# Where SyncE takes the branch over a path that isn't taken: a planned RWKV and expert kernel on one core

## The chip, the cores and the metric

The kernel runs on one core of a Trainium2 chip. The core has a matrix engine (TensorE, "PE" in the profile), three engines for elementwise work (VectorE "DVE", ScalarE "ACT", GpSimd "POOL") and SyncE ("SP"), which in this kernel issues nearly every DMA transfer. Each engine runs its own instructions in order and waits for the others by semaphores. The metric is the device time of one execution in microseconds.

## The reference

Three stages follow each other: a linear attention with decay over the sequence, and two feed-forward stages over the tokens that come out of it.

```python
B, H, S, D = 4, 8, 768, 48
for t in range(S):                                   # attention
    kt, vt, rt = k[:, :, t], v[:, :, t], r[:, :, t]
    cur = einsum('bhd,bhe->bhde', u[None] * kt, vt)
    y[:, :, t] = einsum('bhd,bhde->bhe', rt, state + cur)
    state = w[None, :, :, None] * state + einsum('bhd,bhe->bhde', kt, vt)
x = y.transpose(0, 2, 1, 3).reshape(3072, 384)
h = maximum(maximum(x @ w1, x @ w2), x @ w3)         # 384 -> 768
x = h @ w_out                                        # 768 -> 384
g = x @ w_gate                                       # 384 -> 1536
out = (silu(g) * (x @ w_val)) @ w_out2               # 1536 -> 384
```

All arrays are float32. The decays w are drawn between 0.85 and 0.95.

## The kernel before

The sequence is cut into 6 blocks of 128 tokens; with 4 batch entries there are 24 chunks, numbered n. A chunk of the first block (n below 4) needs no state: its products of queries and keys ("s n"), a masked selection ("select n") and the product with the values ("y n") give its output, and a further product of keys and values ("u n") its contribution to the state. From n = 4 on one step of TensorE, "h n", makes the scores of chunk n and the outputs of chunk n - 1. Between these steps TensorE runs the first feed-forward stage of the blocks that are done ("m i f j", "o i c q") and then the whole second stage ("g", "e").

Each product of a feed-forward stage is made of three passes in a reduced format, from a high and a low part of each operand. The weights are split on the chip, piece by piece (jobs k = 0, 1, ...): "fetch k" brings a piece (SyncE, line 226, into one of three "raw" tiles), "scale k" and "sign k" read it on ScalarE (lines 235, 242), "top k" and "rest k" on VectorE (lines 275, 281; rest k is the last reader of the raw tile, and fetch k + 3 waits for it), "hi k" (ScalarE, line 286) and "lo k" (GpSimd or VectorE, line 289) write the two parts. Pieces 2f and 2f + 1 belong to row f of the first weights, w_a.

The data of a chunk come by SyncE: "load n" brings queries and keys (line 313, four transfers for n from 4 on), scaled by VectorE in "scaled n" (line 352); "rows n" brings keys, values and queries in natural order (line 335, four transfers), used by GpSimd in "bonus n" (lines 365, 366) and "keys n" (line 370). For the first four chunks the keys in natural order come by load_keys (line 341). "sided" (lines 776, 777) copies a table of powers in four transfers, "ub" (line 730) brings u in two, and four transfers (line 725) copy another table into Pz.

The kernel also has a general path for decays outside a range, a loop over the sequence on VectorE that is not taken here. Each engine reads a flag from memory (line 800) and branches over that code (line 801). The flag is made by two instructions of VectorE (lines 780, 781, the step "flag").

The order of all this is not written by hand. A planner (class Plan) holds for each step the engines that can do it, with a cost, its needs, a lag until its result is there, and sometimes an earliest time ("at"). It takes step after step: among those whose needs are planned it takes the one with the least start time less 0.08 times the length of work that depends on it, and calls the function that writes its instructions. Program order on each engine is the order in which the planner took the steps. An engine's first free time stands in the planner's start values; for SyncE it is 20.0. What SyncE issues before that is written ahead of the planner: the loads of the first four chunks, fetch 0 to 2, the copies into Pz, rows 4, the keys of the first four chunks and ub. In the planner those count as there at fixed times:

```python
add(("fetch", k), {"none": 0.0}, [], lambda e: None, at=15.0 + 1.8 * k)
add(("keyed", n), {"none": 0.0}, [("turned",)], lambda e: None, at=20.0 + 0.7 * n)
add(("rows", n), {"none": 0.0}, [], lambda e: None, at=18.0)
```

The step "branch" belongs to no engine. It is taken when the blanked tile, the outputs of the first four chunks, their fills and the flag are planned, and it writes the branch into all five engines at that point of their order. On SyncE the planner had by then placed sided, fetch 3 and load 4.

Of the kernel before, what the change touches and what calls it, by code (L numbers as in the profile page):

```python
# [20 lines left out]
B, H, S, D = 4, 8, 768, 48  # L21
# [69 lines left out]
class Plan:  # L91
# [8 lines left out]


    SHARED = ("top", "rest", "lo", "xlo", "ylo", "prod", "p2", "choose")

# [11 lines left out]
    def run(self, idle, hop=0.1):  # L115
        steps, free = self.steps, self.free
        users, waits = {k: [] for k in steps}, {}
        for key, (_, needs, *_) in steps.items():
# [29 lines left out]
        while ready:  # L148
# [20 lines left out]
            if e == "pe":  # L169
                idle(start - free[e], k)  # L170
            steps[k][2](e)
            free[e] = start + cost
# [11 lines left out]
def rwkv_moe(ctx: ExitStack, tc: tile.TileContext, qk, nat, kn, vn, rn, wcol, wh, uh, wup1, wout1, wup2, out):  # L184
# [459 lines left out]
    with tc.manual_schedule():  # L644
# [77 lines left out]
        for z in range(2):  # L722
            for x in range(2):

                nc.sync.dma_start(out=Pz[64 * z:64 * z + D, 2 * x:2 * x + 2], in_=P129[64 * x:64 * x + D, 2 * z:2 * z + 2])
        load_sides(B)
        for n in range(B):
            load_keys(n)
        for x in range(2):
            nc.sync.dma_start(out=ub[64 * x:64 * x + 64],  # L730
                              in_=uh[NPAIR * x:NPAIR * x + NPAIR].unsqueeze(0).to_broadcast([64, NPAIR, D]))

# [37 lines left out]
        def turned(_):  # L770
            nc.scalar.copy(PT.rearrange("p (j a) d -> p j a d", a=2), late["pt"][:, :, :, 0:D])

        def sided(_):
# [92 lines left out]

        plan = Plan(dict(pe=6.4, dve=5.7, act=6.5, pool=3.3, sync=20.0, none=0.0), order)
        add = plan.add
# [51 lines left out]
        add(("turned",), {"act": 0.5}, [("p", 0)], turned)  # L920
        add(("powers z",), {"act": 0.75}, [("scaled", B - 1)], powers_z, at=16.0)
        add(("sided",), {"sync": 2.0}, [("turned",)], sided, lag=3.0)
        for n in range(B):
            add(("load", n), {"none": 0.0}, [], lambda e: None, at=5.8 + 2.35 * n)
            add(("keyed", n), {"none": 0.0}, [("turned",)], lambda e: None, at=20.0 + 0.7 * n)
            add(("prod", n), {"pool": 1.3} if n > 1 else {"dve": 0.68}, [("load", n)] + ([("d", n - 2)] if n > 1 else []),
                lambda e, n=n: product_columns(n, engine[e]))
            add(("d", n), {"pe": 0.68}, [("prod", n)] + ([("a0", n - 1)] if n else []), lambda e, n=n: diagonal(n))
            add(("scaled", n), {"dve": 1.23}, [("prod", n)], lambda e, n=n: prep_scores(n))
            add(("keys", n), {"pool": 1.03}, [("keyed", n), ("low", B - 1)], lambda e, n=n: prep_keys(n))  # L930
            add(("s", n), {"pe": 1.1}, [("scaled", n)] + ([("select", n - 1)] if n else []), lambda e, n=n: scores(n))
            add(("a0", n), {"act": 0.17}, [("d", n)], lambda e, n=n: bonus(n, engine[e]))
            for x in range(2):
                add(("fill", n, x), {"pool": 1.05, "act": 1.28}, [("a0", n)],
                    lambda e, n=n, x=x: fill(n, x, engine[e]))
            add(("select", n), {"dve": 1.27}, [("s", n), ("fill", n, 0), ("fill", n, 1)], lambda e, n=n: select(n))
            add(("y", n), {"pe": 1.6}, [("select", n)] + {0: [("turned",)], 2: [("low", 0)]}.get(n, bank_free["y", n]),
                lambda e, n=n: apply(n))
            add(("row", n), {"act": 0.48}, [("y", n)], lambda e, n=n: upper(n))
            add(("low", n), {"dve": 0.58}, [("row", n)], lambda e, n=n: lower(n))  # L940
            add(("u", n), {"pe": 0.6}, [("y", n), ("keys", n), ("branch",)] + bank_free["u", n], lambda e, n=n: outer(n))
            add(("update", n), {"act": 0.37}, [("u", n)], lambda e, n=n: update(n))
        for n in range(B, NB * B):
            i, last = n // B, n >= (NB - 1) * B

            done = [("h", n - 1)] if n > B + 1 else []
            add(("load", n), {"sync": 1.9}, done or [("s", n - B)], lambda e, n=n: load_columns(n), lag=2.5,
                at=0.0 if done else 17.0 + 2 * n - 2 * B)
            space = [("rows", B)] if n == B + 1 else [("u", n - B - 2)] if n in (B + 2, B + 3) else [("h", n - 2 if n < 11 else n - 1)] if n > 2 * B else []
            if n > B:  # L950
                add(("rows", n), {"sync": 2.4}, space, lambda e, n=n: load_sides(n), lag=2.5, at=17.0 if n < 2 * B else 40.0)
            else:
                add(("rows", n), {"none": 0.0}, [], lambda e: None, at=18.0)
            add(("bonus", n), {"pool": 2.05}, [("rows", n), ("rest", 2)], lambda e, n=n: prep_bonus(n, engine[e]))
            add(("scaled", n), {"dve": 1.35}, [("load", n), ("low", B - 1), ("lo", 1), ("powers z",)], lambda e, n=n: prep_scores(n))
# [17 lines left out]
        rows0 = [("low", n) for n in range(B)]  # L973
        add(("flag",), {"dve": 0.35}, [("s", 1)], flag, lag=3.0)
        for i in range(2, FAR):
# [157 lines left out]
```

## Time and profile before

| what | value |
|---|---|
| median of 3 runs | 837.82 us (835.02 to 838.01) |
| the profiled execution's own time | 836.52 us |
| its span, first to last instruction | 834.8 us |
| mean granted TensorE clock | 0.995 |
| TensorE busy | 814.4 us, 98% |
| VectorE, ScalarE, GpSimd busy | 362.5, 314.3, 143.0 us |
| moved by DMA | 74.00 MB, 89 GB/s over the span |

The profile is of one execution. Busy times are sums over the span; for TensorE a busy share of 98% leaves 2% of gaps, and where these lie must be read from views with a place or a time. The time of an execution is 1.7 us longer than its span.

### The profile page before, as it was taken

To read this page: it belongs to the slowest core of one execution; us is meant where nothing else is said; L and a number is where in the kernel's file an instruction comes from. 1 tells how busy PE (TensorE), PEld (TensorE's weight loads), DVE (VectorE), ACT (ScalarE), POOL (GpSimd) and SP (SyncE) were. 2 spreads that over 40 slices of the span, in tenths; PEclk is the share of its full clock that TensorE was granted. 3 is DMA by queue.
4 is the path that set the end of the run, shared out by engine and by line. 5 is a ranking of instruction groups with operands and counts; after the bars stand their busy time and mean duration, and the time that the engine had idled before them with its cause. 6 is when DMAs were issued, how large, how long until landed. Compare 5 with 4: busy or idle time off the path is not lost.

```text
span 834.8 us, 14481 instructions
## 1 busy us (share of the span) xinstructions
PE 814.4 (98%) x6058; PEld 673.1 (81%) x6058; DVE 362.5 (43%) x552; ACT 314.3 (38%) x641; POOL 143.0 (17%) x146
## 2 busy tenths in 40 slices
PE   9978899999999999999999999999999999999998
PEld 8756678888888888888888888888888888888886
DVE  7789846747556543234572322222231222213121
ACT  5677753555535432234672211221231122113111
POOL 5763513334343420000121000000000000000000
PEclk9999999999999999999999999999999999999999
DMA  9795725465564462321230100100010010001001
GB/s 268 200 234 147 256 84 146 151 196 166 153 218 136 140 203 104 136 110 58 85 114 1 38 0 1 38 0 1 1 38 0 1 38 0 1 1 39 0 1 38
DMA packets 43787, 74.00 MB, mean 89 GB/s; under 512 B 4584, under 2 KB 30504, under 8 KB 42952
## 3 DMA queue, kind: packets, MB, share of 16 engines
q1 hardware_dynamic: 43712, 73.06, 28.5%
q8 instruction: 47, 0.77, 0.4%
q14 instruction: 20, 0.16, 0.1%
q10 hardware_dynamic: 8, 0.00, 0.0%
HBM read 57.51 MB, written 14.16 MB: 86 GB/s over the span
## 4 chain that ended last, share of the span: by engine, by line
PE 89%; DMA 4%; issue 3%; POOL 2%; SPq 1%; ACT 0%; DVE 0%; POOLq 0%; DVEq 0%; ACTq 0%
PE g L567 12%; PE g L569 12%; PE g L568 12%; PE m L567 8%; PE m L569 8%; PE m L568 7%; PE oo L569 6%; PE oo L567 6%; PE oo L568 6%; PE o L567 3%; PE o L569 3%; PE o L568 3%; PE s L483 2%; PE y L483 2%; DMA raw<-in_wup 1%
## 5 line engine op out<-in xcount | busy, mean ns | idle before, releaser
L567 PE MATMUL g<-xhi,w_c 128*128 128x512 f32 x432 | 168.0, 389 | 0.0
L568 PE MATMUL g<-xlo,w_c 128*128 128x512 f32 x432 | 168.0, 389 | 0.0
L569 PE MATMUL g<-xhi,w_c 128*128 128x512 f32 x432 | 168.0, 389 | 0.0
L624 DVE TENSOR_TENSOR g<-mm,g 128x512 f32<-128x512 f32 x72 | 50.1, 696 | 257.1 <-PE g L569 256.4
L567 PE MATMUL m<-xhi,w_a 128*128 128x512 f32 x324 | 129.6, 400 | 2.0 <-ACT t L235 2.0
L569 PE MATMUL m<-xhi,w_a 128*128 128x512 f32 x324 | 127.6, 394 | 1.5 <-DVE w_a L289 1.3
L568 PE MATMUL m<-xlo,w_a 128*128 128x512 f32 x324 | 127.3, 393 | 0.2 <-DVEq L801 0.2
L620 ACT ACTIVATE mm<-g 128x512 f32<-128x512 f32 x72 | 43.0, 597 | 151.7 <-PE g L569 151.7
L569 PEld LDWEIGHTS g<-xhi,w_c 128*128 128x128 f32 x432 | 81.1, 188 | 16.9
L568 PEld LDWEIGHTS g<-xlo,w_c 128*128 128x128 f32 x432 | 81.1, 188 | 16.8
L567 PEld LDWEIGHTS g<-xhi,w_c 128*128 128x128 f32 x432 | 81.1, 188 | 16.8
L629 ACT CAST gs<-g 128x512 fp32r<-128x512 f32 x72 | 42.2, 587 | 134.0 <-DVE g L624 134.0
L567 PE MATMUL oo<-gs,w_c 128*128 128x512 f32 x216 | 84.0, 389 | 0.0
L568 PE MATMUL oo<-gs,w_c 128*128 128x512 f32 x216 | 84.0, 389 | 0.0
L569 PE MATMUL oo<-gs,w_c 128*128 128x512 f32 x216 | 84.0, 389 | 0.0
L567 PEld LDWEIGHTS m<-xhi,w_a 128*128 128x128 f32 x324 | 61.5, 190 | 15.6 <-ACT t L235 2.1
L569 PEld LDWEIGHTS m<-xhi,w_a 128*128 128x128 f32 x324 | 61.5, 190 | 15.3 <-DVE w_a L289 1.7
L568 PEld LDWEIGHTS m<-xlo,w_a 128*128 128x128 f32 x324 | 61.5, 190 | 12.7 <-DVEq L801 0.5
L601 DVE TENSOR_TENSOR gs<-g,gs 128x512 fp32r<-128x512 f32 x72 | 49.8, 691 | 43.1 <-ACT gs L629 43.1
L598 ACT CAST hs<-m 128x512 fp32r<-128x512 f32 x33 | 19.3, 584 | 78.8 <-DVE m L586 78.8
L568 PEld LDWEIGHTS oo<-gs,w_c 128*128 128x128 f32 x216 | 40.5, 188 | 8.4
L569 PEld LDWEIGHTS oo<-gs,w_c 128*128 128x128 f32 x216 | 40.5, 188 | 8.4
(135 smaller groups left out, 1153.2 us busy)
## 6 DMA issues: line engine op xcount, KB each, us to landing
raw<-in_wup SPq DMA_DIRECT2D x36, 576.0 KB, 4.8
nat<-in_nat SPq DMA_DIRECT2D x80, 144.0 KB, 3.3
aside<-parts SPq DMA_DIRECT2D x12, 576.0 KB, 4.1
w_c<-aside SPq DMA_DIRECT2D x6, 1152.0 KB, 5.8
qk<-in_qk SPq DMA_DIRECT2D x39, 128.0 KB, 3.0
out<-ob SPq DMA_DIRECT2D x18, 256.0 KB, 2.1
qk<-in_qk SPq DMA_DIRECT2D x41, 96.0 KB, 2.7
raw<-in_wout SPq DMA_DIRECT2D x6, 384.0 KB, 3.8
```

The lines of the kernel that those rows point to most:

```text
L483: nc.tensor.matmul(to, w, x, **(how or dict(start=True, stop=True)))
L567: nc.tensor.matmul(p, wh_, xh, start=first, stop=False)
L568: nc.tensor.matmul(p, wh_, xl, start=False, stop=False)
L569: nc.tensor.matmul(p, wl_, xh, start=False, stop=last)
L598: nc.scalar.copy(hsplit[i, f][0], banks["m", i, f, 2])
L601: nc.vector.tensor_tensor(out=g[1], in0=p, in1=g[0].bitcast(F32), op=ALU.subtract)
L620: nc.scalar.activation(out=hs[i, f], in_=banks["g", i, f, 0], func=AF.Silu)
L624: nc.vector.tensor_tensor(out=p, in0=hs[i, f], in1=p, op=ALU.mult)
L629: nc.scalar.copy(t[:, 0], banks["g", i, f, 1])
```

## The change

Four edits belong together.

- SyncE's transfers rows 4, the keys of the first four chunks and ub are no longer written ahead of the planner but are steps of it, with costs on SyncE (2.4, 0.8 each, 0.6) and a lag of 2.5. What needs them waits for them: keys n for keyed n, bonus n for rows n and ub.
- Until the branch is planned, the planner takes SyncE's steps but keeps back their instructions ("held"). When it takes the branch it writes the branch first, and then what was held, in the order in which it was taken. So in SyncE's program order the branch stands directly behind the copies into Pz.
- A step of another engine that needs a step of SyncE also needs the branch (FENCE), so that its instructions are written behind those of the transfer.
- The flag is planned when scaled 0 is, not s 1. SyncE's first free time in the planner is 17.3, not 20.0, and load n from 4 on has no earliest time any more.

```diff
+    FENCE = ("branch",)
...
     def run(self, idle, hop=0.1):
         steps, free = self.steps, self.free
+        held = []
+        for _, (on, needs, *_) in steps.items():
+            if "sync" not in on and any("sync" in steps[d][0] for d in needs):
+                needs.append(self.FENCE)
...
-            steps[k][2](e)
+            if e == "sync" and self.FENCE not in done:
+                held.append((steps[k][2], e))
+            else:
+                steps[k][2](e)
+            if k == self.FENCE:
+                for do, on in held:
+                    do(on)
...
-        load_sides(B)
-        for n in range(B):
-            load_keys(n)
-        for x in range(2):
-            nc.sync.dma_start(out=ub[64 * x:64 * x + 64],
-                              in_=uh[NPAIR * x:NPAIR * x + NPAIR].unsqueeze(0).to_broadcast([64, NPAIR, D]))
...
+        def bring_bonus(_):
+            for x in range(2):
+                nc.sync.dma_start(out=ub[64 * x:64 * x + 64],
+                                  in_=uh[NPAIR * x:NPAIR * x + NPAIR].unsqueeze(0).to_broadcast([64, NPAIR, D]))
...
-        plan = Plan(dict(pe=6.4, dve=5.7, act=6.5, pool=3.3, sync=20.0, none=0.0), order)
+        plan = Plan(dict(pe=6.4, dve=5.7, act=6.5, pool=3.3, sync=17.3, none=0.0), order)
...
+        add(("ub",), {"sync": 0.6}, [], bring_bonus, lag=2.5)
         add(("sided",), {"sync": 2.0}, [("turned",)], sided, lag=3.0)
...
-            add(("keyed", n), {"none": 0.0}, [("turned",)], lambda e: None, at=20.0 + 0.7 * n)
+            add(("keyed", n), {"sync": 0.8}, [], lambda e, n=n: load_keys(n), lag=2.5)
...
-            add(("keys", n), {"pool": 1.03}, [("keyed", n), ("low", B - 1)], lambda e, n=n: prep_keys(n))
+            add(("keys", n), {"pool": 1.03}, [("keyed", n), ("turned",), ("low", B - 1)], lambda e, n=n: prep_keys(n))
...
-            add(("load", n), {"sync": 1.9}, done or [("s", n - B)], lambda e, n=n: load_columns(n), lag=2.5,
-                at=0.0 if done else 17.0 + 2 * n - 2 * B)
+            add(("load", n), {"sync": 1.9}, done or [("s", n - B)], lambda e, n=n: load_columns(n), lag=2.5)
...
-            if n > B:
-                add(("rows", n), {"sync": 2.4}, space, lambda e, n=n: load_sides(n), lag=2.5, at=17.0 if n < 2 * B else 40.0)
-            else:
-                add(("rows", n), {"none": 0.0}, [], lambda e: None, at=18.0)
-            add(("bonus", n), {"pool": 2.05}, [("rows", n), ("rest", 2)], lambda e, n=n: prep_bonus(n, engine[e]))
+            add(("rows", n), {"sync": 2.4}, space, lambda e, n=n: load_sides(n), lag=2.5, at=17.0 if n < 2 * B else 40.0)
+            add(("bonus", n), {"pool": 2.05}, [("rows", n), ("ub",), ("rest", 2)], lambda e, n=n: prep_bonus(n, engine[e]))
...
-        add(("flag",), {"dve": 0.35}, [("s", 1)], flag, lag=3.0)
+        add(("flag",), {"dve": 0.35}, [("scaled", 0)], flag, lag=3.0)
```

## Rows read from the trace of the kernel before

**Rows 1.** The page, part 1: busy time and share of each engine.

```profile
PE 814.4 (98%) x6058; PEld 673.1 (81%) x6058; DVE 362.5 (43%) x552; ACT 314.3 (38%) x641; POOL 143.0 (17%) x146
```

**Rows 2.** Timeline of TensorE: start, length, instruction, idle before it and its releaser.

```profile
36.26 0.50 PE L569 MATMUL m<-xhi,w_a 128*128 128x512 f32 x1 [1.28 <-DVE w_a L289]
...
47.57 0.47 PE L567 MATMUL m<-xhi,w_a 128*128 128x512 f32 x1 [2.04 <-ACT t L235]
...
63.51 0.29 PE L483 MATMUL s<-nat 64*64 64x48 f32 x4 [3.40 <-DVE am L415]
...
106.22 0.37 PE L483 MATMUL y<-am,nat 64*48 64x64 f32 x2 [3.83 <-issue]
```

**Rows 3.** Four stretches: length, busy times, granted clock, DMA share, GB/s.

```profile
15.20:28.00 12.80, 12.61 (x157) 10.35 (x154) 10.69 (x15) 10.67 (x24) 8.89 (x8) 1.00 0.80 211
28.00:32.50 4.50, 4.50 (x22) 3.72 (x21) 4.47 (x5) 2.65 (x4) 4.50 (x4) 1.00 0.43 107
32.50:61.40 28.90, 24.10 (x323) 18.45 (x321) 20.92 (x30) 19.36 (x50) 17.99 (x14) 0.94 1.01 239
112.00:800.00 688.00, 688.00 (x4682) 569.81 (x4681) 266.41 (x399) 235.37 (x460) 84.13 (x83) 1.00 0.22 71
```

**Rows 4.** Timeline of SyncE's DMA issues.

```profile
8.16 4.35 SPq L725 DMA_DIRECT2D Pz<-P  x4
12.56 4.96 SPq L335 DMA_DIRECT2D nat<-in_nat  x4
17.56 2.59 SPq L341 DMA_DIRECT2D kv<-in_nat  x4
20.19 1.13 SPq L730 DMA_DIRECT2D ub<-in_uh  x2
...
24.64 0.52 SPq L226 DMA_DIRECT2D raw<-in_wup  x1
25.26 2.54 SPq L313 DMA_DIRECT2D qk<-in_qk  x4
31.52 0.34 SPq L226 DMA_DIRECT2D raw<-in_wup  x1
...
35.21 2.49 SPq L313 DMA_DIRECT2D qk<-in_qk  x4
```

**Rows 5.** Line 800, the flag read: engine, length in ns, first and last start.

```profile
L800 SPq TENSOR_LOAD <-slow_i x1: 722/722/722, 27.9 to 27.9; - x1
```

**Rows 6.** Line 801, the branch, in the same columns.

```profile
L801 SPq EVENT_SEMAPHORE  x8: 17/17/17, 29.5 to 31.4; - x8
...
L801 DVEq EVENT_SEMAPHORE  x1: 21/21/21, 27.0 to 27.0; - x1
```

**Rows 7.** DMA issues from 25.2 to 27.8: KB each, median us to landing.

```profile
qk<-in_qk SPq DMA_DIRECT2D x2, 128.0 KB, 4.1
qk<-in_qk SPq DMA_DIRECT2D x2, 96.0 KB, 4.1
```

**Rows 8.** Timeline of VectorE.

```profile
10.32 1.32 DVE L417 COPY_PREDICATED am<-mask,s 128x1024 f32<-128x1024 uint8 x1 [1.15 <-ACT am L403]
...
25.81 1.17 DVE L281 SCALAR_TENSOR_TENSOR t<-raw,t 128x576 uint16<-128x576 uint32 x1
...
31.42 1.26 DVE L352 TENSOR_TENSOR qk<-qk,powers_z 112x512 f32<-112x512 f32 x2
...
35.47 0.74 DVE L289 TENSOR_TENSOR w_a<-t,w_a 128x576 fp32r<-128x576 f32 x1
...
43.41 1.29 DVE L352 TENSOR_TENSOR qk<-qk,powers_z 112x512 f32<-112x512 f32 x2 [6.14 <-DMA qk<-in_qk]
44.61 0.75 DVE L275 SCALAR_TENSOR_TENSOR t<-t,signs 128x576 uint32<-128x576 uint32 x1
```

**Rows 9.** The chain that ended last, up to 26 us: start, length, what.

```profile
5.97 9.18 DMA raw<-in_wup
...
23.81 2.48 POOL kv L370 x2
```

**Rows 10.** The tile Pz: its transfers from issue to landing.

```profile
DMA to landing us min/median/max: 6.0/7.4/9.0
```

## The prediction

> **What bounds the kernel now.** I read the page first. TensorE is busy for 814.4 of the 834.8 us [rows 1], so only its gaps can give time back, 20.4 us in all. TensorE's instructions in order of time show the large ones behind the first up product [rows 2]: 1.3 us in front of an up product at 36.26, waiting for a weight; 2.0 us in front of one at 47.57; 3.4 us in front of a state step at 63.51; 3.8 us, called issue, that end at 106.22. From 112 to 800 us it is busy without a gap (the fourth of [rows 3]), so a microsecond that TensorE gains before that is a microsecond of the total, and one that it doesn't gain is nothing.
>
> Next the other stretches of that view, for DMA and the clock [rows 3]. From 32.5 to 61.4 us the DMA share is 1.01: the engines are full. Before that they aren't: 0.80 over 12.8 us and 0.43 over the 4.5 us from 28.0 to 32.5, which is 2.6 us unused in each. The granted clock of 32.5 to 61.4 is 0.94, so some products there run at the lower level (1.2 GHz): 28.9 x 0.06 = 1.7 us, behind the 2.0 us gap.
>
> Then SyncE's queue in order of time [rows 4]. It issues with little rest up to 27.8 us, and then nothing until 31.52, when fetch 4 goes out, although the tile that fetch 4 refills was read for the last time at 26.98 (rest 1 on VectorE, 25.81 + 1.17, [rows 8]). The hole is the branch: SyncE loads the flag at 27.9 [rows 5] and its eight semaphore events run from 29.5 to 31.4 [rows 6]. The last transfers before the hole are load 4's four, issued 25.26 to 27.80 and landing 4.1 us after issue each [rows 4, 7]: from 29.4 to some 31.4. The events start and end just there. So I read the hole as SyncE, inside the branch that isn't taken, waiting until each of its outstanding transfers has landed.
>
> Last, VectorE [rows 8]: it stands 6.14 us from 37.27 to 43.41 for load 5, which SyncE issued at 35.21. Behind it in VectorE's order are top 4 (44.61) and rest 4, then hi 4 and lo 4, the weight of the up product that starts at 47.57. That is the chain from the hole to TensorE: branch, fetch 4, rows 5, fetch 5, load 5, scaled 5, top 4, lo 4, TensorE.
>
> **The change, part by part.** *The flag* is planned after scaled 0, not after s 1: its two instructions, among VectorE's smallest, move ahead of select 0, in front of which VectorE idles 1.15 us at 10.32 [rows 8]. That wait hides them; without it they would cost their own length once, the same that they cost now. I take 0.
>
> *SyncE's branch* comes right behind the four Pz transfers. Their issues end at 12.5. From the flag's load to the first event took 1.6 us (27.9 to 29.5), so the events begin near 14.1; then SyncE must see raw 0 to 2 and Pz land. Raw lands at 15.15 [rows 9]. Pz landed 6.0 to 9.0 us after issue, the last one (issued 12.0) at about 18.0 [rows 10], but then with nat's transfers behind it on the engines. So SyncE is through between 15.2 and 18.1; I take 17.0, nearer to the upper end, since Pz queues behind raw.
> The Trainium skill, page "Runtime: NRT & Kernel Launch", Instruction fetch mechanics, says that a taken branch to code outside the fetched pages must first fetch it by DMA. By that rule the step from 12.5 to the first event could be longer here than at 28 us, since the engines are full at 13 us; no row of before shows SyncE branching under load, and the sum would stay within the upper end.
>
> *What is now behind it.* By the planner's weights I expect this order from 17.0: rows 4 (four transfers, 2.54 us as load 4 took), keys 0 and 1 (half of 2.59), ub 1.13, fetch 3 0.52, the four sided transfers (from the end of ub at 21.3 to 24.6, 3.3), load 4 2.54 [rows 4]: 11.3, with the gaps between issues 11.5. Fetch 4 then goes out at 28.5, not at 31.52: 3.0 us sooner. With 15.2 and 18.1 in place of 17.0 it is 4.5 (rest 1's own limit as well) and 1.9 sooner. Keys 2 and 3 probably follow rows 5 and take the 1.3 us that they no longer take before load 4, so load 5 is 1.7 to 3.0 us sooner. Before, rows 4 took 4.96 us for the same four issues, being held up by full engines; that time now passes inside the branch. This is why a wait of 3.6 us moved to a start 4.4 us later still gains.
>
> *The other engines.* Steps that need a transfer of SyncE must follow the branch. Everything so bound already stood behind it: VectorE's event is at 27.0 [rows 6], and keys 0 on GpSimd at 23.81 [rows 9] is the earliest such step. Cost 0, since the transfers land in time: rows 4 are issued by 19.5 and keys 0 by 20.2, and at the 4.1 us of load 4 they are there by 24.3, which is 0.5 us late for keys 0 at worst, and GpSimd idles for several microseconds before lo 3. Load 4 is the tight one: its last transfer is issued at about 28 and lands near 31.7, where scaled 4 starts at 31.42 [rows 8]. Between 1.5 us sooner and 1.4 later (P at 15.2 and 18.1), and lateness goes on to lo 2 (35.47 to 36.21, [rows 8]), for which TensorE already waits 1.3 us. I take 0.3 lost, which the 2.0 us gap absorbs.
>
> *What TensorE gets.* If load 5 lands 1.7 to 3.0 us sooner, the 2.0 us gap that begins at 45.5 is gone or nearly so, and with it most of the 1.7 us of low clock: TensorE can be 2 to 3.7 us ahead at 51.7. The next gap, 3.4 us before 63.51, waits for load 6. That one is issued when h 5 has run on TensorE, so it moves along, but it lands through full engines. How far ahead they are is bounded by the share they leave unused. Before: 5.2 us up to 32.5. After: about 1.5 idle until P, and 2.3 MB issued over 11.5 us is 202 GB/s against 239 GB/s when full [rows 3], so 0.15 x 11.5 = 1.8 unused; together 3.3 to 3.8. That leaves 1.4 to 1.9 us from this side and 3.0 from the issue side.
> The Trainium skill, page "Trainium Kernel Development and Optimization", Key Constraints, speaks against the change: transfers of all queues share the same 16 engines, and other ways of issuing only save the sequencer's time. By that rule the gain would be the 1.4 us of share recovered; by the issue side alone 3.0.
> Behind 61.4 the engines are no longer full, and what is gained stays. I take 2.5 us, between the two sides and nearer to the issue side, since the 2.0 us gap itself hangs on load 5, ahead of most of the full stretch.
>
> Sum: the profiled execution took 836.52 us (span 834.8 and 1.7 around it); 836.5 - 2.5 = **834.0 us**. The median of the runs shown is 1.3 us above the profile; on its scale it is 835.3.
>
> **The rivals.**
> *Bigger.* VectorE's order changes: in the new plan load 5 is due later, so top 4 and rest 4 may stand ahead of scaled 5. Then w_a2 waits for no load, fetch 7 (behind rest 4) goes out up to 5 us sooner, the backlog in front of load 6 is less, and part of the 3.4 us gap goes too: 2.0 + 1.7 + up to 3.4 = 7, or 829.5 to 832. For it: load 5's lateness is the planner's error in before. Against: load 6 still waits for h 5. The issue gap of 3.8 us before 106.22 is the other piece that could go if TensorE reaches it while the engines are less full; it hangs on relative timing that the change hardly touches.
> *Nothing.* The full engines give back all of it: load 6 lands as late as now, and TensorE waits 5 us there. For it: share 1.01 until 61.4. Against: 2.6 us unused just at the hole. 836 to 837.
> *Slower.* SyncE's events aren't waits for its own transfers but for the other engines to be through their branch. VectorE's event is at 27.0 [rows 6], so SyncE would stand from 14 to 27 with nothing in flight, and fetch 4 would be issued at 38.5, 7 us later than now: 841 to 845. It decides from the point at which SyncE leaves after 20.0 (31.5 less 11.5). For it: VectorE was through before SyncE's first event. Against: GpSimd works behind its branch at 23.81 [rows 9], before VectorE has come to its own; and the four waits match four landings. A milder form with the same sign is keys 2 and 3 running on GpSimd at 35 beside rest 3 and lo 2 on VectorE, 2.5 us for the pair as for keys 0 and 1 [rows 9]; it costs 1 to 2 us at the 1.3 us wait.
>
> **How the numbers follow.** Forecast 0.44, bigger 0.30, nothing 0.12, slower 0.14. About 0.5%, 4.2 us, is what a measurement of this kernel can tell from no change. Of the forecast's own range (832 to 835.5) a tenth lies beyond that, so faster 0.34, same 0.52, slower 0.14. The range leaves out the strongest bigger case and the slower one: 829.5 to 838.
>
> **What would show it.** SyncE's flag load near 12.6 us and its events ending by 18.1, with no hole at 28; fetch 4 near 28.5; VectorE's wait for load 5 shorter than 4.5 us, or top 4 ahead of it; no TensorE gap before 47.57 and no products at the lower clock behind it; the gap before h 6 still there. The prediction is wrong if SyncE's events end near 27, if scaled 4 starts after 33, or if the gap before h 6 grows by what the one before it lost.

## The result and the profile after

The changed kernel takes 829.8 us (median of 5 runs, 828.58 to 831.98), the kernel before 837.82 us in the same series (835.02 to 839.17). The ratio is 0.9914, with a 95% interval of 0.9888 to 0.994: about 7 us faster. The profiled execution took 829.47 us, its span is 827.8 us. So 7.0 us are to be found between the two traces.

Part 1 of the page after, to be read beside [rows 1]:

```profile
PE 811.8 (98%) x6058; PEld 671.1 (81%) x6058; DVE 361.1 (44%) x550; ACT 314.8 (38%) x645; POOL 143.8 (17%) x147
```

TensorE is busy 2.6 us less for the same 6058 instructions, since fewer of them run at the lower clock, and idle 4.4 us less (16.0, was 20.4). The timeline of TensorE after has these large gaps up to h 6, in the columns of [rows 2]; from 100 to 112 us it shows none:

```profile
36.66 0.50 PE L581 MATMUL m<-xhi,w_a 128*128 128x512 f32 x1 [1.99 <-DVE w_a L301]
...
46.43 0.47 PE L579 MATMUL m<-xhi,w_a 128*128 128x512 f32 x1 [0.52 <-DVE h L598]
...
53.48 0.50 PE L581 MATMUL m<-xhi,w_a 128*128 128x512 f32 x1 [1.39 <-DVE w_a L301]
...
57.99 0.50 PE L581 MATMUL m<-xhi,w_a 128*128 128x512 f32 x1 [0.77 <-DVE w_a L301]
...
62.44 0.42 PE L495 MATMUL s<-nat 64*64 64x48 f32 x4 [2.56 <-POOL nat L377]
```

The 2.0 us gap of before is down to 0.52, the one ahead of h 6 to 2.56, and the 3.83 us inside h 9 (called issue) are gone. Two waits for weights between h 5 and h 6, 1.39 and 0.77 us, are new. A fourth gap of before, ahead of h 8, is gone too; it ended 0.10 us behind a step of VectorE (a "select", line 415), which after runs 4.75 us sooner, ahead of other work:

```profile
82.27 0.71 DVE L415 COPY_PREDICATED am<-mask,s 128x512 f32<-128x512 uint8 x1
...
83.08 0.25 PE L483 MATMUL s<-nat 64*64 64x48 f32 x2 [1.20 <-issue]
```

```profile
77.52 0.74 DVE L427 COPY_PREDICATED am<-mask,s 128x512 f32<-128x512 uint8 x1
```

Where TensorE stood at the same step of its work, from the start times of these timelines, gives the ledger (us; "not held" is an experiment below):

```
step                         before   after   lead   not held, 2nd   its lead
h 4                           38.09   38.47   -0.4       39.84         -1.8
h 5                           51.70   48.67    3.0       49.82          1.9
h 6                           63.51   62.44    1.1       63.66         -0.2
h 7                           73.48   73.14    0.3       74.40         -0.9
h 8                           83.08   81.56    1.5       82.82          0.3
h 9                          100.32   98.94    1.4       99.78          0.5
first up product behind h 9  106.52  100.94    5.6      101.79          4.7
h 10                         120.41  113.41    7.0      114.26          6.2
```

At h 7 the lead is down to 0.3 us; 1.2 us come with the gap ahead of h 8, so that 1.4 us are there at h 9. 4.2 us come inside h 9 and 1.4 us behind it: 5.6 us in a place that the forecast left as it was. These are two executions, and one kernel's executions differ by as much as the early leads: a second profile of the kernel before reached h 7 at 76.40 and h 9 at 103.80. Over the profiles of all experiments below (without the two with added transfers), h 7 starts at 73.48 to 76.40 in the old order and at 72.72 to 74.79 in the new one, so a lead there isn't shown. The gap ahead of h 8 (1.08 to 1.52 us) stands in all five profiles of the old order and in none of the new one. The stages, in the columns of [rows 3]; the third row here is a new one:

```profile
15.20:28.00 12.80, 12.80 (x158) 10.64 (x157) 10.09 (x13) 10.52 (x24) 7.05 (x7) 1.00 0.59 167
28.00:32.50 4.50, 4.50 (x21) 3.73 (x20) 4.02 (x4) 2.75 (x4) 3.74 (x3) 1.00 0.64 156
...
16.50:20.10 3.60, 3.60 (x50) 3.09 (x48) 2.28 (x4) 3.02 (x9) 0.94 (x1) 1.00 0.00 1
...
32.50:61.40 28.90, 22.72 (x321) 17.19 (x320) 23.22 (x32) 20.22 (x51) 16.19 (x14) 1.00 1.01 260
100.00:112.00 12.00, 12.00 (x118) 10.03 (x109) 7.60 (x15) 8.31 (x20) 2.66 (x2) 1.00 0.61 198
112.00:800.00 688.00, 688.00 (x4682) 569.78 (x4681) 265.79 (x397) 235.29 (x459) 83.36 (x82) 1.00 0.22 71
```

SyncE's hole hasn't vanished, it has moved: from 16.5 to 20.1 us the DMA engines move nothing at all. What they leave unused from 15.2 to 32.5 us is 12.8 x 0.41 + 4.5 x 0.36 = 6.9 us, against 5.1 before. The low clock of 32.5 to 61.4 is gone from there, but a stretch of it stands behind the gap ahead of h 6, where the kernel before had the full clock (the first line is of after, the second of before):

```profile
62.44:65.80 3.36, 3.36 (x126) 3.36 (x128) 3.22 (x5) 1.76 (x3) 3.36 (x4) 0.50 0.07 22
```

```profile
62.00:66.00 4.00, 2.49 (x130) 2.40 (x131) 3.97 (x8) 1.88 (x4) 0.00 (x0) 1.00 0.29 112
```

So of the two stretches at the lower level that the kernel before has up to 112 us, one moved and one went: in 100 to 112 the clock was 0.86 before, with 8.17 us busy of 12, and is 1.00 after:

```profile
100.00:112.00 12.00, 8.17 (x148) 6.50 (x147) 4.80 (x9) 5.03 (x12) 2.15 (x3) 0.86 0.60 198
```

SyncE's DMA issues after [rows 4], and its flag read and events, with VectorE's event [rows 5, 6]:

```profile
8.11 4.03 SPq L737 DMA_DIRECT2D Pz<-P  x4
18.64 2.60 SPq L347 DMA_DIRECT2D nat<-in_nat  x4
21.29 1.07 SPq L353 DMA_DIRECT2D kv<-in_nat  x2
22.41 1.12 SPq L781 DMA_DIRECT2D ub<-in_uh  x2
23.65 0.50 SPq L238 DMA_DIRECT2D raw<-in_wup  x1
24.20 1.49 SPq L787 DMA_DIRECT2D PT<-PT  x1
...
27.70 2.79 SPq L325 DMA_DIRECT2D qk<-in_qk  x4
30.60 0.52 SPq L238 DMA_DIRECT2D raw<-in_wup  x1
31.17 2.51 SPq L347 DMA_DIRECT2D nat<-in_nat  x4
33.73 1.07 SPq L353 DMA_DIRECT2D kv<-in_nat  x2
34.90 0.36 SPq L238 DMA_DIRECT2D raw<-in_wup  x1
35.37 2.52 SPq L325 DMA_DIRECT2D qk<-in_qk  x4
```

```profile
L811 SPq TENSOR_LOAD <-slow_i x1: 742/742/742, 12.2 to 12.2; - x1
...
L812 SPq EVENT_SEMAPHORE  x8: 17/17/17, 18.0 to 18.6; - x8
...
L812 DVEq EVENT_SEMAPHORE  x1: 21/21/21, 26.7 to 26.7; - x1
```

The order is the one of the forecast, the start isn't: rows 4 at 18.64, fetch 4 at 30.60, load 5 at 35.37 (35.21 before). Load 4's transfers take 3.4 and 2.8 us to land, against 4.1 [rows 7]:

```profile
qk<-in_qk SPq DMA_DIRECT2D x2, 128.0 KB, 3.4
qk<-in_qk SPq DMA_DIRECT2D x2, 96.0 KB, 2.8
```

VectorE after, around its wait for load 5 [rows 8]: lo 3, top 4, rest 4, and then scaled 5:

```profile
37.58 0.75 DVE L301 TENSOR_TENSOR w_a<-t,w_a 128x576 fp32r<-128x576 f32 x1
38.24 0.76 DVE L287 SCALAR_TENSOR_TENSOR t<-t,signs 128x576 uint32<-128x576 uint32 x1
39.03 1.49 DVE L293 SCALAR_TENSOR_TENSOR t<-raw,t 128x576 uint16<-128x576 uint32 x1
44.14 1.28 DVE L364 TENSOR_TENSOR qk<-qk,powers_z 112x512 f32<-112x512 f32 x2 [3.62 <-DMA qk<-in_qk]
```

Load 5 is there 0.7 us later than before. The wait is shorter because three instructions moved in front of it; before, top 4 stood behind it at 44.61. The chain that ended last no longer reaches back to 26 us [rows 9]; it starts with an issue gap at 90.74 and this row:

```profile
90.83 0.57 DVE w_b L301
```

Pz lands about as long after its issue as before [rows 10]; its last transfer, issued at 11.64, lands at 18.02:

```profile
DMA to landing us min/median/max: 6.4/7.6/8.7
```

### The profile page after: what moved, and what is told of

The parts are those of the page before. It is cut to its first block, busy times and chain, and to the rows that moved or that the text cites. A ratio compares the mean times of both kernels' runs of the same rounds, so it can differ in the third digit from the quotient of the medians.

```text
span 827.8 us, 14490 instructions
## 1 busy us (share of the span) xinstructions
PE 811.8 (98%) x6058; PEld 671.1 (81%) x6058; DVE 361.1 (44%) x550; ACT 314.8 (38%) x645; POOL 143.8 (17%) x147
## 4 chain that ended last, share of the span: by engine, by line
PE 89%; ACT 0%; DVE 0%; issue 0%
PE g L579 12%; PE g L580 12%; PE g L581 12%; PE m L579 8%; PE m L580 7%; PE m L581 7%; PE oo L579 6%; PE oo L581 6%; PE oo L580 6%; PE o L581 3%; PE o L579 3%; PE o L580 3%; PE s L495 2%; PE y L495 2%; ACT ob L653 0%; DVE w_b L301 0%
## 5 line engine op out<-in xcount | busy, mean ns | idle before, releaser
L581 PEld LDWEIGHTS m<-xhi,w_a 128*128 128x128 f32 x324 | 60.8, 188 | 18.1 <-DVE w_a L301 5.4
```

The lines of the kernel that those rows point to most:

```text
L581: nc.tensor.matmul(p, wl_, xh, start=False, stop=last)
```

## The experiments

Each ratio is to the kernel before in the same series, with its 95% interval.

**A second profile of the kernel before** (no edit), to see whether the gap inside h 9 is an accident of one execution.

> The kernel before, unchanged, for a second profile. Theory C (most of the difference is a gap of TensorE of 3.8 us at 102.4 that belongs to the kernel before): the gap is there again, 3 to 4.5 us long inside the tenth chunk's step, with a block of TensorE's code landing at its end and products at the lower clock behind it; span 834 to 837. Rival (the gap was an accident of one execution): no gap at 102, span 829 to 831.

The gap is there again: 3.55 us ahead of 109.43, called issue (841.02 us, one execution).

**The old order with the early branch.** Only SyncE's program differs from the kernel before; the order planned for the other engines is untouched.

```diff
+            if e == "sync" and ("branch",) not in done:
+                held.append((steps[k][2], e))
...
-        load_sides(B)
-        for n in range(B):
-            load_keys(n)
...
+        plan.first = first_transfers     # rows 4, keys 0 to 3, ub: first of what was held
```

> The kernel before with SyncE's branch directly behind the copies into Pz, and rows 4, the keys, ub, sided, fetch 3 and load 4 behind it in the old order; every other engine's program is that of before. Theory A (the early branch pays by itself): fetch 4 goes out 1 us or more sooner than at 31.52 and TensorE is at least 1 us ahead at 98 us; 1 to 2 us less if the gap at 102 stays, 6 to 7 less if it goes. Theory B (the planner's new order on VectorE and GpSimd gave what was gained before 98 us): SyncE leaves the branch near 18.6 to 19.5, fetch 4 goes out near 31.5 as before, nothing is gained: 836 to 838, with the gap at 102 still there.

838.6 us; ratio 1.0014 (1.0003 to 1.0025). Its SyncE and TensorE timelines:

```profile
18.49 2.61 SPq L342 DMA_DIRECT2D nat<-in_nat  x4
...
31.16 0.52 SPq L233 DMA_DIRECT2D raw<-in_wup  x1
...
34.97 4.13 SPq L320 DMA_DIRECT2D qk<-in_qk  x4
```

```profile
106.53 0.27 PE L490 MATMUL y<-am,nat 64*48 64x64 f32 x2 [3.22 <-issue]
```

The hole at 28 us is gone, yet fetch 4 is only 0.4 us sooner and load 5 0.2: the time has been spent at 16 to 19.9 us, where the DMA share is 0.01. And the gap inside h 9 stays. In the old order the early branch is worth nothing. (The flag is planned as late as before here: SyncE takes the compare at 17.36, behind the last landing at 17.03, and its events end at 18.4.)

**The new order with the late branch** (SyncE's part of the branch between sided and load 4, as planned), run twice.

```diff
-            if e == "sync" and self.FENCE not in done:
-                held.append((steps[k][2], e))
-            else:
-                steps[k][2](e)
+            steps[k][2](e)
```

> The changed kernel with SyncE's branch written where the planner takes it (behind sided, ahead of load 4); every other engine's program is that of the changed kernel. Theory B: VectorE has the fourth weight piece ahead of load 5 as in the changed kernel, the step h 5 starts within 1 us of 48.7, and the time is within 1.5 us of the changed kernel's 829.8. Theory A: the hole of SyncE's branch is back near 25 us, load 5 lands 2 us later or more, h 5 and all behind it 1.5 us or more later, 831.5 to 833; with the gap at 102 back as well, 836 to 838.

> The changed kernel with SyncE's part of the branch back at its planned place, between the transfers into PT2 and load 4, timed once more (its first run gave a ratio of 0.9933 to the kernel before; four kernels with the early branch and this order gave 0.9896 to 0.9918). Nothing is left out. Theory (the early branch is worth 1 to 2 us in the new order): the ratio is 0.993 to 0.9945 again, and steps 4 and 5 start 1 to 1.6 us later than in the changed kernel. Rival (the early branch is worth nothing, as in the old order, and the first run caught a stretch of low clock): the ratio is 0.990 to 0.992.

832.15 us, ratio 0.9933 (0.9911 to 0.9954), and 832.49 us, ratio 0.9952 (0.9935 to 0.9969). The second ratio lies outside both of its expected ranges, nearer to that of the theory. So the order alone gives some 4 to 5.5 us of the 7, and the gap inside h 9 is gone without the early branch. The first profile had a stretch of low clock at 92 to 100 us (granted 0.50 to 0.72, the level of 1.2 GHz); the second had none, and its VectorE runs in the same order as after:

```profile
45.30 1.29 DVE L361 TENSOR_TENSOR qk<-qk,powers_z 112x512 f32<-112x512 f32 x2 [3.41 <-DMA qk<-in_qk]
```

Scaled 5 is 1.16 us later than after, h 5 1.15, h 9 0.84. By the medians the early branch is worth some 2.5 us in the new order, by series that weren't run side by side. Neither shows it: the two profiles of this one kernel have h 9 at 103.80 and 99.78, and the intervals of the ratios (0.9888 to 0.994 with the early branch, 0.9911 to 0.9954 and 0.9935 to 0.9969 without) overlap. What the early branch is worth in the new order stays open, between nothing and some 3 us.

**The copies moved away, in the old order.** In h 9 the DMA engines carry three copies of 768 KB, which SyncE issues behind a second branch (their direction is y<-x). Here they are cut to 16 columns and made whole behind h 10.

```diff
-                    nc.sync.dma_start(out=y, in_=x2[FAR - 1])
+                    nc.sync.dma_start(out=y[:, 0, 0:16], in_=x2[FAR - 1][:, 0, 0:16])
...
+        add(("wiped",), {"sync": 6.0}, [("choose", 1), ("h", 2 * B + 2)], wipe, lag=2.5)
```

> The kernel before with the three copies of 768 KB into the far buffers reduced to 16 columns in the second branch, and made whole behind the step h 10, outside of a branch (so they would spoil the general path's results, which these inputs don't take); every other engine's program is that of before. Theory C: the gap at 102 and the low clock behind it are gone and nothing else changes: 5 to 5.5 us less, 831 to 833. Rival (the gap comes from the second branch itself, or from the loads of weights beside it): the gap stays within 1 us of 3.8 and the time within 1 us of before.

833.12 us; ratio 0.995 (0.9933 to 0.9968), some 4 us less by the ratio, not 5 to 5.5. The gap shrinks to

```profile
104.50 0.27 PE L483 MATMUL y<-am,nat 64*48 64x64 f32 x2 [0.54 <-issue]
```

What TensorE waits for there is code. DMA queue q8 brings it in packets of 16 KB; q1 carries SyncE's transfers. In the kernel before no packet of q8 runs from 96 to 103.9 us, in which q1 moves 2.93 MB; the next one is in the window 103.92 to 104.94, when TensorE has been dry since 102.4:

```profile
q8 instruction: 1, 0.02, 5.8%
```

After, the packet that stands at that place of the program starts at 96.5 us, 2.4 us ahead of h 9. With the copies moved away it starts at 102.1, before TensorE runs dry at 103.96. In all five profiles with a gap inside h 9 TensorE goes on 2.3 to 2.4 us behind the start of this packet, whether it starts at 101.3 or at 107.1. So the 3.8 us are a block of TensorE's code that comes late, and the copies have a part in that.

**Where TensorE's second branch stands.** The programs of TensorE before and after differ in one thing, apart from a few waits: the second branch stands nine o products earlier after. Three kernels place it later in the new order, or later still in the old one. The other engines' orders change by a few neighbours of the branch.

```diff
-add(("choose", 1), ..., [("repack", 1)], second_branch, lag=0.4)
+add(("choose", 1), ..., [("repack", 1), ("o", 0, 0, 0)], second_branch, lag=0.4)   # new order, 18 products later
```

> The changed kernel, but TensorE's second branch (the one that picks the copies into y_far) comes behind the first group of nine products of o, as in the order of before, and SyncE's three copies then come behind the three loads of wout instead of ahead of them. Nothing is left out. Theory (the 3.8 us gap inside h 9 comes from the place of the second branch in TensorE's program and of the transfers around it, and the early branch of SyncE has no part in it): the code block that TensorE needs inside h 9 is fetched later than 98 us, a gap of 3 to 4 us marked issue is back inside h 9 near 100 to 106, with a lower granted clock behind it, and the time is 833 to 836, that is 3 to 6 us above the changed kernel's 829.8. Rival (the gap went because TensorE reaches h 9 at another time, or because of VectorE's and POOL's new order): no gap over 1 us inside h 9, block fetched ahead of it, time 829 to 832.

```diff
+    ... (out1(i, c, fs), second_branch(e) if ("o", i, c, q) == ("o", 0, 0, 0) else None)   # new order, 9 later
```

> The changed kernel with the second branch of all engines one group of nine products of o later, which puts it in TensorE's program exactly where the kernel before has it (the run with two groups later showed no gap inside h 9). Nothing is left out; VectorE's, ScalarE's and POOL's orders differ by a few neighbours of the branch, and two loads of wout go out ahead of the three copies. Theory E (the gap inside h 9 hangs on where that branch stands in TensorE's program: at this one place the code block for h 9 is fetched 3 to 6 us after the products that fetch it in time in the other programs): the block is fetched only when TensorE has run dry, a gap of 3 to 4 us marked issue is back inside h 9, with a lower clock behind it, and the time is 833 to 836. Rival (timing: it hangs on the copies and on when TensorE comes to h 9, not on the place): no gap over 1 us inside h 9 and 829 to 832.

The same edit with ("o", 0, 1, 0) in the kernel before puts the branch 9 products later than there:

> The kernel before with the second branch of all engines one group of nine products of o later, where the run with two groups later has it in TensorE's program; one load of wout moves ahead of the copies, and some neighbours of the branch on the other engines change places. Nothing is left out. Theory E (the place of the branch): the block for h 9 is fetched ahead of it, the gap of 3.8 us inside h 9 is gone, the granted clock behind it stays full, and the time falls by 4 to 6 us, to 832 to 834. Rival (timing of copies and of TensorE): the gap stays at 3 to 4 us, and the time within 1.5 us of 837.5.

Measured, with the start of the code packet less the start of h 9, both from the trace (negative: the packet comes first):

```
kernel                       ratio (interval)           packet less h 9            gap inside h 9
before                       1                          103.94 - 100.32 =  3.6     3.83
before, early branch         1.0014 (1.0003, 1.0025)    104.24 - 101.23 =  3.0     3.22
before, copies late          0.995  (0.9933, 0.9968)    102.10 - 101.89 =  0.2     0.54
before, branch 9 later       0.9974 (0.9957, 0.9991)    101.30 - 101.03 =  0.3     0.64
after, branch as in before   0.9947 (0.993, 0.9963)      99.58 - 100.50 = -0.9     none
after, branch 18 later       0.9911 (0.9881, 0.994)      99.92 - 102.08 = -2.2     none
after                        0.9914 (0.9888, 0.994)      96.50 -  98.94 = -2.4     none
after, late branch, 1st      0.9933 (0.9911, 0.9954)    100.53 - 103.80 = -3.3     none
after, late branch, 2nd      0.9952 (0.9935, 0.9969)     96.45 -  99.78 = -3.3     none
```

My theory that the place of the second branch decides alone fell: at before's place, in the new order, no gap came back. The rival, that the gap stays as it is wherever the branch stands, fell too: moving it in the old order took the gap from 3.83 to 0.64 us in the profile. But this edit also puts a load of wout ahead of the copies and starts these at 95.07, not at 93.85, so it doesn't tell the place of the branch from the timing of the copies. That kernel's 12 runs spread from 831.76 to 839.4 us, so the late fetch probably comes in some executions only; this wasn't profiled. What holds is that the packet comes sooner with each of the three edits (copies away, branch later, new order), and that TensorE has a gap in every profile in which the packet starts behind h 9, and in none of the others. What in the order sets the packet's time stays open. The two medians of 833.3 and 835.6 us for the moved branches are above what their profiles show (831.03 and 832.5 us), so their gain by the profile isn't the gain of all executions.

**Rows 8 behind load 6**, which changes SyncE's program alone, apart from a few waits: the place where the lead of 3.0 us at h 5 shrinks to 1.1 at h 6.

```diff
-  ... else [("h", n - 2 if n < 11 else n - 1)] if n > 2 * B else []
+  ... else [("h", n - 2 if n < 11 else n - 1)] if n > 2 * B else [("h", B + 1)] if n == 2 * B else []
```

> The changed kernel, with SyncE's row transfers of step 8 moved from ahead of load 6 to behind it; every other engine's program is the same. Nothing is left out. Theory (the DMA engines are full from 32 to 61 us and SyncE issues one transfer after another, so what stands ahead of load 6 sets when step 6 starts; this is the place where the lead of 3.0 us at step 5 shrank to 1.1): load 6 is issued 3 to 4 us sooner (about 49 instead of 52.8), TensorE's gap before h 6 (2.56 us) shrinks to under 1 us, h 6 starts 1.5 to 2 us sooner, and the time falls by 0.5 to 2 us, to 828 to 829. Rival (the lead is given back to whatever is late next: rows 8 land late for step 8, or the loads are slower): h 6 starts sooner, a new gap of 1 to 2 us stands ahead of h 7 or h 8, and the time stays within 0.5 us of 829.8 or above it.

829.09 us; ratio 0.9896 (0.9864 to 0.9929). TensorE ahead of h 6:

```profile
63.28 0.29 PE L495 MATMUL s<-nat 64*64 64x48 f32 x4 [1.68 <-DMA nat<-in_nat]
```

What was expected of h 6 didn't come: load 6 went out at 53.32 (52.82 after), not near 49, the gap is 1.68 us, not under 1, and h 6 starts 0.8 us later than after. In this execution SyncE left the branch 1.7 us later and h 5 started at 51.28, 2.6 us later than after. From h 5 to h 6 it needs 12.0 us, against 13.8 after. That isn't the work of the edit, as far as the runs tell: the kernel with the branch in before's place, which has rows 8 where they were, needs 11.3 us (52.61 to 63.94), with an h 5 that is later still. So it isn't shown that the transfers ahead of load 6 took the lead back. At h 9 (97.76) this kernel is 1.2 us ahead of after. The median is 0.7 us below the changed kernel's, which these intervals don't separate; it is the fastest version measured.

**What SyncE's events wait for.** One kernel moves the Pz copies to ScalarE's queue. Two add transfers that nothing uses, on SyncE's queue or on ScalarE's.

```diff
-                nc.sync.dma_start(out=Pz[...], in_=P129[...])         # SyncE at 8.1 us
+                    nc.scalar.dma_start(out=Pz[...], in_=P129[...])   # behind ScalarE's copy of PT
```

> The changed kernel, with the four copies into Pz issued by ScalarE behind its copy of PT (about 13 us) instead of by SyncE at 8.1; every other instruction is where it was. Nothing is left out. Theory (an engine that passes the branch waits until the transfers that it issued itself have landed; SyncE's last ones are now fetch 2 at 7.8 instead of Pz at 12.1): SyncE's events on the branch's line end 2 to 4 us sooner, at 14 to 16 instead of 18.6, rows 4 start at about 15, fetch 4 goes out at 27 to 29 instead of 30.6, and the time falls by 0 to 1.5 us. Rival (the events wait for something else, such as the flag's way to the other engines or code that is fetched): they still end at 18 to 18.6, and nothing moves by more than 0.5 us.

```diff
+        for z in range(2):                                            # 2 x 576 KB, DRAM to DRAM
+            nc.sync.dma_start(out=junk[z], in_=jobs[z][3].bitcast(U32))     # or nc.scalar, behind PT
```

> The changed kernel with two transfers more, 576 KB each, from DRAM to DRAM and used by nothing, issued by SyncE behind Pz and ahead of the branch. Nothing is left out. Theory (SyncE passes the branch only when the transfers that it issued itself have landed): its events on the branch's line start 2 to 4 us later, at 20 to 22 instead of 18.0, about 1 to 2 us behind the last packet of these transfers. Rival (the events wait for the flag's read and the code behind the branch alone): they start within 1.5 us of 18.0, well ahead of the last packet.

> The same two transfers, issued by ScalarE behind its copy of PT instead of by SyncE. Nothing is left out. Theory (only SyncE's own transfers count): SyncE's events start at 18 to 19.5, ahead of the last packet on ScalarE's queue, which lands at 19 to 22. Rival (any queue's transfers, or engines that are full, hold the events): they start behind the last packet of ScalarE's queue, as with SyncE's own.

The lines of the branch, in the three kernels in this order:

```profile
L815 SPq EVENT_SEMAPHORE  x8: 17/17/17, 18.1 to 18.6; - x8
```

```profile
L815 SPq EVENT_SEMAPHORE  x8: 17/17/17, 19.9 to 23.6; - x8
```

```profile
L815 SPq EVENT_SEMAPHORE  x8: 17/17/17, 21.5 to 22.1; - x8
```

What the events wait for can be read from the trace itself. Each of the eight waits for one of eight semaphores and then adds to it, and on these semaphores the transfers count their landings, 16 counts to a transfer. Set beside the last count ahead of it (us):

```
kernel                   event   starts   last count   of the transfer
before                   2nd      30.25      30.24     load 4, by SyncE at 25.89
after                    1st      18.03      18.02     Pz, by SyncE at 11.64
Pz on ScalarE            1st      18.08      18.07     Pz, by ScalarE at 13.55
added, SyncE             1st      19.86      19.84     Pz, by SyncE at 14.17
added, SyncE             2nd      21.08      21.06     added, by SyncE at 14.72
added, SyncE             3rd      23.23      23.21     added, by SyncE at 15.86
added, ScalarE           1st      21.53      21.51     Pz, by SyncE at 12.23
```

In the 14 profiles 34 of the 112 events start 0.02 to 0.04 us behind the last count on their semaphore, five (each the first of its kernel) 0.5 us behind the compare, and the other 73 within 0.10 us of the event before. So they are waits for landings, and neither for the other engines (VectorE's event is at 26.5 with the transfers added on SyncE) nor, but for those five, for the flag's read.

And they aren't waits for SyncE's own transfers alone, which was the theory. With Pz on ScalarE, SyncE takes the compare at 9.5 us, 3.8 us sooner than after, and the last of its own transfers (fetch 2) has landed at 16.95; the first event still starts at 18.08, 0.02 us behind the landing of the last Pz transfer, which ScalarE issued:

```profile
L780 ACTq DMA_DIRECT2D Pz<-P x4: 594/602/603, 11.6 to 13.6; - x4
...
DMA to landing us min/median/max: 4.5/5.0/5.5
```

That is why the expected gain didn't come (830.19 us, ratio 0.9918 (0.9885, 0.9951)). In the run with transfers added on ScalarE, SyncE's own Pz packets were held up to 21.07, and its first event waited for them. Both runs with added transfers are of one execution (833.46 and 833.78 us).

## Why the prediction was partly right

**The flag, the order on SyncE, the reading of the hole: right.** The order behind the branch came word for word. The events are waits for landings, of the last transfer on each of eight semaphores, whichever engine issued it, and the rival *slower* (a wait for the other engines until 27) is excluded.

**P, the time at which SyncE is through: mis-sized.** I took 17.0 from bounds of 15.2 and 18.1; it was 18.6. My upper bound was the landing of the last Pz transfer, and that is what decided: it landed at 18.02. I went below it because nat's transfers would no longer be on the engines behind Pz, and that sped Pz up by nothing that shows (median 7.6 us from issue to landing, 7.4 before). The eight events themselves took 0.6 us more, for which I had no term.

**Fetch 4 and load 5: mis-sized with it.** Fetch 4 came 0.9 us sooner, not 3.0: 1.6 of the missing 2.1 are P, and 0.5 the sequence (12.0 us, not 11.5). Load 5 came 0.2 us later, not 1.7 to 3.0 us sooner: keys 2 and 3 in front of it take another 1.1.

**The DMA side: wrong in sign.** I counted 1.5 us of idle DMA engines until P and so 1.4 to 1.9 us recovered. They idled 3.6 us, and up to 32.5 they left 1.7 us more unused than before. The Trainium skill, page "Trainium Kernel Development and Optimization", Key Constraints, says that the transfers of all queues run on the same 16 DMA engines and that issuing from several engines at once only saves issue time. That the early branch alone moved nothing (ratio 1.0014) fits with that, though the page doesn't speak of the order on one queue.

**The 2.0 us gap and the low clock: right in what, wrong in why.** Both went from where they stood, and the lead of 3.0 us at h 5 lies in the forecast's 2 to 3.7. But load 5 didn't bring it. VectorE's order did, with top 4 and rest 4 ahead of scaled 5: the first half of the rival *bigger*. The gap isn't in every execution of the old order either: three of its five profiles have it (2.04, 2.01 and 2.68 us), the second one of the kernel before doesn't. And the low clock came back behind h 6 (0.50 from 62.44 to 65.80).

**The give-back: mis-sized.** I kept 2.5 us and wrote that behind 61.4 what is gained stays. 1.1 us were left at h 6, after two new waits for weights, and 0.3 at h 7, after the low clock: of what the forecast was added up from, next to nothing. The 1.2 us of VectorE's select ahead of h 8 I had no term for.

**The gap of 3.8 us inside h 9: the step that failed.** I wrote that it "hangs on relative timing that the change hardly touches". It was 5.6 of the 7.0 us. It is late code, and the planner's new order touches everything around it: which transfers stand in front of the copies, and where TensorE's second branch is. I had put it in the rival *bigger*, whose 829.5 to 832 holds the result; the likeliest case, 834.0, was 4.5 us above the profiled execution. That the range holds the result, at its very edge, is luck: the sum of *bigger* (2.0 + 1.7 + up to 3.4) isn't what happened either, and this gap stands in it only as another piece that could go. The Trainium skill, page "Runtime: NRT & Kernel Launch", Instruction fetch mechanics, calls the cost of crossing a block of code "mostly hidden"; in the three profiles of TensorE's old program with the copies in place it wasn't (3.83, 3.55 and 3.22 us), in those of the new order it was. The same section's warning, that a taken branch breaks the fetch ahead, fits the place behind a branch; the runs don't show that this is the cause.

Worked out from the two profiles, the 7.0 us are then: 0.3 up to h 7, 1.2 at h 8, where VectorE's select comes in time, 0.1 lost up to h 9, and 5.6 from the code that comes in time. The gaps at h 8 and in h 9 went in every profile of the new order, with the early branch or without; what the early branch adds isn't settled by these runs.

## What to carry to other kernels

In this kernel SyncE's side of a branch that isn't taken held eight waits for landings, so it wasn't free while transfers were under way, its own or another engine's. Moved to an earlier place it moved the stall, and what that saves is read from the DMA engines' idle time before and after, not from the hole that went. What such a wait is for can be read by setting its start beside the last count on its semaphore. A gap called issue on TensorE deserves a look at the code queue's packets beside it; if a block comes late there, another order of the transfers or branches nearby may remove it, as it did here. When a change goes through a planner, run the new order without the change, and the change in the old order, before the time is credited to either; and take a second profile of the same kernel, before a lead of a microsecond or two is explained.

## What the runs showed of the hardware

- A block of TensorE's code of 16 KB came 3.0 to 3.6 us behind the start of the step that needs it in the old order and 0.9 to 3.3 us ahead of it in the new one, and when it was late it cost 3.2 to 3.8 us of gap and, in the kernel before, 1.4 us behind it. TensorE went on 2.3 to 2.4 us behind the start of the late packet (five profiles). After, it came amid the packets of the 768 KB copies (92.3 to 99.7 us) with a DMA share of 1.08 from 96 to 98, so full DMA engines alone don't explain a late one.
- A transfer counted 16 times on its semaphore, and an event that waited for it started 0.02 to 0.04 us behind the last count (34 events in 14 profiles). After, the last packet of SyncE's queue ended at 16.51 and the last count came at 18.02; the eight events took 0.6 us. The DMA engines stood still for 3.6 us meanwhile (share 0.00 from 16.5 to 20.1).
- The same four transfers of rows 4 took 4.96 us to issue at 12.6 us [rows 4], when the DMA share was 1.04 (11.0 to 15.2 us), and 2.60 us at 18.6 us, when it was 0.00.
